# Three PSUM banks in turn for halves of the output products, maximum and bias in one VectorE operation, and another order of elements in the multiplication by the softmax reciprocals

## The chip, the core and the metric

The kernel runs on one core of one Trainium2 chip. A core has TensorE for matrix products (its results go to PSUM, 8 banks of 512 float32 per partition), VectorE, ScalarE and GpSimd for elementwise work, and SyncE, which here only issues transfers. The time is the device time of the core in microseconds; a profiled execution also gives its span, from the first to the last instruction.

## What is computed

One transformer block on 2048 rows of 576 numbers, with modulation by a conditioning vector:

```python
mod = (silu(c) @ w_mod).reshape(1, 6, 1, 576)
sa, ca, ga, sb, cb, gb = mod[:, 0], mod[:, 1], ...
h = layernorm(x) * (1 + ca) + sa
x = x + ga * attention(h)      # 32 query heads on 16 cached key/value heads, the last 512 positions
h = layernorm(x) * (1 + cb) + sb
x = x + gb * ((silu(h @ w1) * (h @ w3)) @ w2)   # 4608 hidden columns
```
In attention each query head's scores (2048 x 512) go through a softmax, are multiplied by the values, and the heads' outputs are multiplied by `wo` (4096 x 576) and summed.

## The kernel before

Everything is computed in pairs of float16 numbers, a high half and the rest: each matrix product is three products (high by high, high by low, low by high). The 2048 rows are four blocks of 512. Attention is a list of 128 slots `i`, each one query head on one block; a slot has four steps `t`, one for each tile of 128 rows. The main loop (from L1599) writes down the instructions of all engines step by step, each engine works its list in order, and the framework adds the waits between engines. In a step of slot `i` TensorE's list has:

- the scores of tile `t` (`scores`, three products of 512 columns, L508), in one of two banks tagged `S`;
- a third of the next slot's query projection (`query`, L435 and L439), in one of two banks tagged `A`;
- a part of the output products of two heads that were finished earlier (`attend_out`, `back`, L458);
- at times four transposes of normalized rows (`turn_rows`, L257) or small products of one column.

At the end of the slot come the twelve products of the probabilities of slot `i - 1` with the values (`values`, L587).

**Softmax.** VectorE takes the negated maximum of the scores (L512) and turns it into the bias of the exponential (L513), ScalarE computes the exponential from PSUM with this bias (`weights`, L525). The probabilities are split into halves by ScalarE (L557) and GpSimd (L562) and turned by a transposing transfer; the fourth tile is turned by TensorE (`turn`, L548) into a bank tagged `T`, and VectorE makes its low half (`turn_low`, L577). The reciprocals of the row sums go to memory and come back spread over the partitions as `r`, with the four tiles of a row next to each other. `normalize` (L596) multiplies the head's output `po` by them on VectorE, two slots later, at step 1; at step 3 ScalarE and GpSimd split the result (`split_on`, L606 and L607).

**Output products.** The two query heads of a key head make a pair. Its four tiles take eight steps: one for the first head (six products, both halves of the 576 columns, L458), one for the second, which adds to it. Then VectorE multiplies by a factor and adds the tile to the accumulated rows `acc` (L617). PSUM has two banks `E` for this, one for each half of the columns, so that the first product of a tile waits for the accumulate of the tile before. Small sums of peaks use free columns of the second bank (`sum_peaks`, `in_total`, `out_total`), and VectorE copies them out (L336, L1170, L1199). After the last slot `E` and a second pair of banks, in the place of `T`, take turns.

**Other uses of T.** Two banks `T` in turn serve the fourth tile and the transposes of normalized rows: for the first block before the loop (with banks `A` and `S`), for the second in the first steps (`make_h` with `early`), for the third and fourth within slots 8 to 12 and, for the second layer norm of the first two blocks, in slots 112 to 116 (`store_h`). ScalarE or VectorE reads each of them with gain and shift (L266, L268, L270, L272, L284, L286, L656). The very first query product, of slot 0, uses the first bank of `E` (`project_first`, L445 to L451).

The attention slots end at about 1590 us; then the feed-forward part runs (L874, L959). Its code stays as it is, apart from the bank and columns of the small sums.

Of the kernel before, what the change touches and what calls it, by code (L numbers as in the profile page):

```python
# [48 lines left out]
def tile_block(  # L49
# [47 lines left out]
    sc = const.tile([P, DC + 4], F32, name="sc")  # L97
    low_rows = sc[:, DC + 3 :]
# [41 lines left out]
    ones = const.tile([P, P], F32, name="ones")  # L140
    nc.gpsimd.memset(ones, 1.0)
    peak_cols = const.tile([P, 12], BF16, name="peak_cols")
# [17 lines left out]
    def mod_cols(wm, name, one, tag):  # L160

        ps = t_bank() if tag == "T" else bank(tag, f"ps_{name}")
# [12 lines left out]
    def mod_rows(wm, kind):  # L175

        vec = gate_rows[kind]
        wm = wm[0]
        for h in range(2):
            for d in (0, 3):  # L180
                nc.tensor.matmul(
                    E[:, h, :HALF], ones, wm[:, d, h * HALF : (h + 1) * HALF], start=d == 0, stop=d == 3
                )
        nc.vector.tensor_copy(half_split(vec), E[:, :, :HALF])
        return vec
# [67 lines left out]
    def turn_rows(b, m, tag):  # L253

        ps = t_bank() if tag == "T" else bank(tag, "ps_n")
        for t in range(ST):
            nc.tensor.transpose(ps[:, t * P : (t + 1) * P], norms[b][1][t][:, m * P : (m + 1) * P], ident)  # L257
        return ps
# [51 lines left out]
    factors = const.tile([P, HKV, 3], F32, name="factors")  # L310
# [17 lines left out]
    def sum_peaks(g, lo, hi, ps=None):  # L328

        ps = E[:, 1, 400:416] if ps is None else ps  # L330
        nc.tensor.matmul(ps[:, lo:hi], peak_ones, tops[g][:, lo:hi], start=True, stop=True)

    def take_sums(g, lo, hi, ps=None):

        ps = E[:, 1, 400:416] if ps is None else ps
        nc.vector.tensor_copy(peaks[g][:, 5 + lo : 5 + hi], ps[:, lo:hi])  # L336

    def score_factors(g):
        down = peaks[g][:, 5:10]
        nc.vector.tensor_scalar(  # L340
            factors[:, g, 0:2], down[:, 0:2], down[:, 2:3], score_down, op0=ALU.mult, op1=ALU.mult
        )
# [110 lines left out]
    def back(ps, o, w, t, first, last):  # L453

        rows = slice(t * P, (t + 1) * P)
        for n, (x, y) in enumerate(((0, 0), (0, 1), (1, 0))):
            for h in range(2):
                nc.tensor.matmul(  # L458
                    ps[:, h, :HALF],
                    o[:, x, rows],  # L460
                    w[:, y, h * HALF : (h + 1) * HALF],
                    start=first and n == 0,
                    stop=last and n == 2,
                )
# [35 lines left out]
    def scores(i, t):  # L500
        u, j, b = slots[i]
        g = uses[u][0]
        st = state[i]
        k, q = keys[u], st["qT"]
        rows = slice(t * P, (t + 1) * P)
        pss = bank("S", "pss")
        for n, (x, y) in enumerate(((0, 0), (0, 1), (1, 0))):
            nc.tensor.matmul(pss, q[:, x, rows], k[:, y, :], start=n == 0, stop=n == 2)  # L508
        m = (i * ST + t) % 3
        nm = nms[:, 2 * m : 2 * m + 2]  # L510
        factor = factors[:, g, j : j + 1]
        nc.vector.tensor_reduce(nm[:, 0:1], pss, axis=AX.X, op=ALU.max, negate=True)  # L512
        nc.vector.tensor_scalar(nm[:, 1:2], nm[:, 0:1], factor, P_LOG, op0=ALU.mult, op1=ALU.add)  # L513
        st["max", t] = pss, nm

    def weights(i, t):

        u, j, b = slots[i]
        factor = factors[:, uses[u][0], j : j + 1]
        st = state[i]  # L520
        pss, nm = st.pop(("max", t))
        if t == 0:
            st["l"] = odd.tile([P, 2 * ST], F32, tag="l", name="l", bufs=3)
        p = pool.tile([P, SB], F32, tag="p", name="p", bufs=PB)
        nc.scalar.activation(p, pss, AF.Exp, bias=nm[:, 1:2], scale=factor, accum_out=st["l"][:, t : t + 1])  # L525
        st["p", t] = p
# [15 lines left out]
    def turn(i, t):  # L542
# [3 lines left out]
        ps = st["t"] = t_bank().rearrange("p (j n) -> p j n", j=KC)  # L546
# [45 lines left out]
    def normalize(i):  # L592
# [16 lines left out]
    def attend_out(pair, t, j, total):  # L609
        u, _, b = slots[2 * pair]  # L610
        lane[0] += j == 0
        ps = spare()
        back(ps, state[2 * pair + j]["o"], wos[u][:, j], t, j == 0, j == 1)
        if j == 1:
# [3 lines left out]
                a, ps[:, :, :HALF], factors[:, uses[u][0], 2:3], a, op0=ALU.mult, op1=ALU.add  # L618
# [4 lines left out]
    for pair in range(n // 2):  # L623
        for k in range(2 * ST):
# [6 lines left out]
            outs.setdefault(when, []).append((pair, *divmod(k, 2)))  # L631
# [17 lines left out]
    def store_h(b, m, tag, tag_out):  # L649
# [9 lines left out]
        store_later(hd[b][m * P : m * P + n, :], hf[:n], ("s", b, m) if tag == "T" else None)  # L659
# [448 lines left out]
    def scale_first(ps):  # L1108
# [15 lines left out]
        nc.gpsimd.tensor_scalar(score_down, small[:, 5:6], SCALE / Q_DOWN, None, op0=ALU.mult)  # L1124
# [20 lines left out]
    lane = [0, ()]  # L1145

# [12 lines left out]
    def in_total(f):  # L1159

        m = peak_cols[:, 4 * (f % 2) :][:, :4]
        for part in range(2):
            peak = m[:, 2 * part + 1 : 2 * part + 2]
            nc.tensor.matmul(
                spare()[:, 1, 408:410], peak.to_broadcast([P, P]), m[:, 2 * part : 2 * part + 2],
# [3 lines left out]
    def in_taken(f):  # L1169
        nc.vector.tensor_copy(stats[:, f, :], spare()[:, 1, 408:410])  # L1170
# [24 lines left out]
    def out_total(p):  # L1195
        nc.tensor.matmul(spare()[:, 1, 410:411], peak_ones, peak_cols[:, 8 + p % 2 : 9 + p % 2], start=True, stop=True)

    def out_taken(p):
        nc.vector.tensor_copy(out_down[:, p : p + 1], spare()[:, 1, 410:411])  # L1199
# [236 lines left out]
    def make_h(b, m, early=False):  # L1436
        modulate(hT[b], m, turn_rows(b, m, "T"), vecs["shift", "a"], vecs["gain", "a"], early)
# [88 lines left out]
    at(106, 2, make_cols, "shift", "b", 3, 0.0, "T")  # L1526
    at(109, 2, make_cols, "gain", "b", 4, 1.0, "T")
    at(109, 3, lambda: spread_peaks("b", mlp_small))
    at(110, 1, lambda: scale_cols("b", t_bank(), mlp_small, 2.0**-8))
# [24 lines left out]
    turned = [turn_rows(0, m, "TTAAS"[m]) for m in range(DC + 1)]  # L1554
# [44 lines left out]
    for i in range(n + 2):  # L1599
        run(i, -1)  # L1600
        for t in range(ST):
# [121 lines left out]
```

## Time and profile before

| what | us |
|---|---|
| three runs of the kernel before: median (lowest to highest) | 2752.52 (2752.24 to 2756.41) |
| the profiled execution | 2752.42 |
| its span | 2750.3 |

In the profile's lines PE is TensorE, PEld its weight loads, DVE VectorE, ACT ScalarE, POOL GpSimd. A group's line has the source line, the engine, the operation, what it writes and reads by the program's names, the shapes and the count, then the busy time, the mean of one in ns, and the idle time of the engine just before with what ended it. A line of the list of waits has the waiting engine, tile and line, what it waited for, the total in us, how often, and the longest. A timeline line has its start, its length, and in brackets the wait before it. Products are pipelined: the end of one is modelled and lies behind the start of the next. In the table by stretches of time each line has its bounds, its length, and then the busy time of TensorE, its weight loads, VectorE, ScalarE and GpSimd.

### The profile page before, as it was taken

How to read it: one execution, taken by the hardware profiler on the slowest of the kernel's cores; microseconds unless marked ns; L12 is line 12 of the kernel's file. 1: busy time of each engine (PE TensorE's matmuls, PEld its weight loads, DVE VectorE, ACT ScalarE, POOL GpSimd, SP SyncE). 2: the span in 40 equal slices, each digit the busy share in tenths (PEclk: the TensorE clock that was granted, in tenths of full speed). 3: DMA queues.
4: the chain of work that ended last, by engine and by line, in shares of the span. 5: the costliest groups of instructions: out<-in, count | busy, mean ns of one | idle time of the engine just before them, and what ended most of it. 6: DMA issues, size and time to landing. Idle time of an engine off the chain costs nothing.

```text
span 2750.3 us, 44762 instructions
## 1 busy us (share of the span) xinstructions
PE 2682.3 (98%) x15406; PEld 1511.8 (55%) x15406; DVE 1995.2 (73%) x3550; ACT 1622.9 (59%) x3026; POOL 1873.1 (68%) x1745
## 2 busy tenths in 40 slices
PE   6899999999999999999999999999999999999998
PEld 3455555555555555555555555555555555555555
DVE  7877787878787787887876667777776666566566
ACT  6776778777777778777677635544443323333332
POOL 4677888888888877777669637688774465334435
PEclk9999999999999999999999999999999999999999
DMA  6778888778787888978879945656643434333332
GB/s 196 174 171 198 195 180 192 168 182 188 171 187 165 190 193 193 214 178 208 194 182 219 241 134 171 200 165 201 208 160 107 157 122 129 102 103 111 105 109 85
DMA packets 593460, 463.84 MB, mean 169 GB/s; under 512 B 442704, under 2 KB 472528, under 8 KB 592208
## 3 DMA queue, kind: packets, MB, share of 16 engines
q1 hardware_dynamic: 592944, 460.69, 65.4%
q8 instruction: 121, 1.98, 0.3%
q14 instruction: 107, 0.88, 0.1%
q10 hardware_dynamic: 288, 0.30, 0.0%
HBM read 264.19 MB, written 95.99 MB: 131 GB/s over the span
## 4 chain that ended last, share of the span: by engine, by line
PE 50%; DVE 2%; POOL 2%; issue 1%; DMA 1%; ACT 1%; SPq 0%; POOLq 0%; DVEq 0%; ACTq 0%
PE py L874 15%; PE px L874 11%; PE pf L959 6%; PE pe L959 6%; PE pe L458 3%; PE po L587 3%; PE pss L508 2%; PE pq L435 2%; DMA r<-row 1%; PE pt L548 0%; POOL acc L913 0%; PE pq L439 0%; DMA row<-l 0%; DVE table L512 0%; POOL sums L913 0%
## 5 line engine op out<-in xcount | busy, mean ns | idle before, releaser
L562 POOL TENSOR_TENSOR hp<-p,hp 128x512 f16<-128x512 f32 x384 | 448.8, 1171 | 269.6 <-ACT hp L557 154.1
L525 ACT ACTIVATE p<-pss,table,factors 128x512 f32<-128x512 f32 x512 | 396.8, 775 | 355.1 <-DVE table L513 175.7
L874 PEld LDWEIGHTS <-wset 128*128 128x128 f16 x3528 | 344.2, 98 | 337.4 <-issue 4.0
L512 DVE TENSOR_REDUCE table<-pss 128x1 f32<-128x512 f32 x512 | 350.3, 684 | 199.4 <-PE pss L508 198.8
L874 PE MATMUL py<-hset,wset 128*128 128x512 f16 x2016 | 482.1, 379 | 0.0
L458 PE MATMUL pe<-o 128*128 128x288 f16 x3024 | 453.4, 286 | 11.6 <-DVE acc L617 10.7
L508 PE MATMUL pss<-k,qT 128*128 128x512 f16 x1536 | 418.0, 380 | 13.2 <-ACT p L525 10.6
L458 PEld LDWEIGHTS <-o 128*128 128x128 f16 x3072 | 300.8, 98 | 186.1 <-issue 17.5
L587 PE MATMUL po<-ptw,v 128*128 128x512 f16 x1536 | 358.6, 381 | 7.8 <-DVE ptw L577 2.7
L874 PE MATMUL px<-hset,wset 128*128 128x512 f16 x1512 | 361.5, 379 | 2.1 <-ACT p L525 2.1
L94 POOL TENSOR_TENSOR akv<-u,akv 128x512 f16<-128x512 f32 x141 | 164.8, 1178 | 178.4 <-ACT akv L93 170.5
L435 PE MATMUL pq<-hT,wq 128*128 128x512 f16 x1092 | 280.6, 379 | 0.0
L557 ACT CAST hp<-p 128x512 f16<-128x512 f32 x384 | 237.3, 618 | 14.1 <-DMA ptw<-hp 0.9
L587 PEld LDWEIGHTS <-v 128*128 128x128 f16 x1536 | 147.8, 98 | 175.0 <-issue 16.2
L959 PEld LDWEIGHTS <-akv 128*128 128x128 f16 x1728 | 169.1, 98 | 89.3 <-issue 0.8
L508 PEld LDWEIGHTS <-qT 128*128 128x128 f16 x1536 | 147.6, 98 | 127.2 <-issue 14.8
L617 DVE SCALAR_TENSOR_TENSOR acc<-pe,factors,acc 128x576 f32<-128x576 f32 x252 | 204.3, 811 | 4.8 <-PE pe L458 4.8
L607 POOL TENSOR_TENSOR o<-on,o 128x512 f16<-128x512 f32 x128 | 150.2, 1174 | 54.0 <-ACT o L606 52.0
L435 PEld LDWEIGHTS <-wq 128*128 128x128 f16 x1092 | 106.9, 98 | 127.4 <-issue 1.0
L953 DVE SCALAR_TENSOR_TENSOR acc<-pf,table,acc 128x576 f32<-128x576 f32 x140 | 113.5, 811 | 79.3 <-PE pf L959 79.3
L1052 ACT COPY u<-py 128x512 f32<-128x512 f32 x72 | 42.2, 586 | 201.3 <-PE py L874 199.4
L1045 ACT ACTIVATE s<-s,table 128x512 f32<-128x512 f32 x72 | 52.0, 722 | 175.1 <-DVE s L1044 175.0
(254 smaller groups left out, 4789.0 us busy)
## 6 DMA issues: line engine op xcount, KB each, us to landing
wset<-wd SPq DMA_DIRECT2D x213, 320.0 KB, 3.2
r<-row SPq DMA_DIRECT2D x128, 256.0 KB, 3.9
oset<-od SPq DMA_DIRECT2D x106, 288.0 KB, 3.2
wraw<-in_w SPq DMA_DIRECT2D x36, 768.0 KB, 5.5
wd<-wmade SPq DMA_DIRECT2D x75, 320.0 KB, 3.2
wset<-wd SPq DMA_DIRECT2D x71, 160.0 KB, 2.2
w2raw<-in_w SPq DMA_DIRECT2D x19, 576.0 KB, 5.2
wd<-ring SPq DMA_DIRECT2D x33, 320.0 KB, 2.8
```

The costliest lines, as they stand in the source:

```text
L94: eng.tensor_sub(halves[:, 1], src, halves[:, 0])
L435: nc.tensor.matmul(ps, w[:, k // 2, m, :], hT[:, DC + m if k == 1 else m, :], start=s == 0, stop=False)
L458: nc.tensor.matmul(ps[:, h, :HALF], o[:, x, rows], w[:, y, h * HALF : (h + 1) * HALF], start=first and n == 0, stop=last and n == 2,)
L508: nc.tensor.matmul(pss, q[:, x, rows], k[:, y, :], start=n == 0, stop=n == 2)
L512: nc.vector.tensor_reduce(nm[:, 0:1], pss, axis=AX.X, op=ALU.max, negate=True)
L525: nc.scalar.activation(p, pss, AF.Exp, bias=nm[:, 1:2], scale=factor, accum_out=st["l"][:, t : t + 1])
L557: nc.scalar.copy(hp[:, 0, :], state[i]["p", t])
L562: nc.gpsimd.tensor_sub(hp[:, 1, :], state[i].pop(("p", t)), hp[:, 0, :])
L587: nc.tensor.matmul(po, v[:, x, c, :], pt[:, y, c, :], start=c == 0 and n == 0, stop=c == KC - 1 and n == 2)
L617: nc.vector.scalar_tensor_tensor(a, ps[:, :, :HALF], factors[:, uses[u][0], 2:3], a, op0=ALU.mult, op1=ALU.add)
L874: nc.tensor.matmul(ps, w[:, a, :], h[:, b, :], start=start and n == 0, stop=stop and n == 6, skip_group_check=True)
L959: nc.tensor.matmul(ps[:, h, :HALF], a[:, rows], w[:, b, :], start=m == 0, stop=m == 2)
```

## The change

1. **Three banks.** `E` is now one tile of three banks. The lower half of the columns always goes to bank 0, the upper half to bank 1 and 2 in turn (`lane[0]`, flipped by each tile). The tile `T` has one buffer instead of two. What else used `T` uses a bank of `E`: banks 1 and 2 at the start, later the one that is idle at the time (`idle()`). The small sums move to free columns of bank 0. After the last slot the two pairs `pe` and `pf` are new tiles.
2. **The order of the output products.** A step does one half of the columns for both heads (six products), the upper half first, instead of both halves for one head.
3. **One operation for maximum and bias.** L512 and L513 become one VectorE operation that adds a constant to each score, multiplies by the negated factor, takes the minimum over the row as an accumulator, and also writes the products themselves as bytes to a tile that nobody reads. It needs two more factors for each head, made at the same place as the old one.
4. **The multiplication by the reciprocals** runs over the same elements in another order: the four tiles innermost, so that `r` is read in its order in memory, and `po` and `on` in steps of 128 elements.
5. The matrix of ones is one column, read as if it were 128.

```diff
-    E = psum.tile([P, 2, 512], F32, tag="E", name="pe", bufs=1)
     turning = ExitStack()
-    tpool = turning.enter_context(tc.tile_pool(name="tpool", bufs=2, space=PSUM))
-
-    def t_bank():
-        return tpool.tile([P, 512], F32, tag="T", name="pt")
+    tpool = turning.enter_context(tc.tile_pool(name="tpool", bufs=1, space=PSUM))
+    E = tpool.tile([P, 3, 512], F32, tag="E", name="pe")
+    lane = [1, ()]
+
+    def both_halves():
+        return lane[1][lane[0] % 2][:, :, :HALF] if lane[1] else E[:, 0 : lane[0] + 1 : lane[0], :HALF]
+
+    def idle():
+        return E[:, 3 - lane[0], :]
...
-        ps = t_bank() if tag == "T" else bank(tag, "ps_n")
+        ps = idle() if tag == "E" else E[:, int(tag), :] if tag in "012" else bank(tag, "ps_n")
         for t in range(ST):
...
-    def back(ps, o, w, t, first, last):
+    def back(ps, o, w, t, h, first, last):
...
         for n, (x, y) in enumerate(((0, 0), (0, 1), (1, 0))):
-            for h in range(2):
-                nc.tensor.matmul(
-                    ps[:, h, :HALF],
-                    o[:, x, rows],
-                    w[:, y, h * HALF : (h + 1) * HALF],
-                    start=first and n == 0,
-                    stop=last and n == 2,
-                )
+            nc.tensor.matmul(
+                ps,
+                o[:, x, rows],
+                w[:, y, h * HALF : (h + 1) * HALF],
+                start=first and n == 0,
+                stop=last and n == 2,
+            )
...
-        nc.vector.tensor_reduce(nm[:, 0:1], pss, axis=AX.X, op=ALU.max, negate=True)
-        nc.vector.tensor_scalar(nm[:, 1:2], nm[:, 0:1], factor, P_LOG, op0=ALU.mult, op1=ALU.add)
+        nc.vector.tensor_tensor_reduce(
+            spent, pss, to_log.to_broadcast([P, W]), turned, 3.0e38, op0=ALU.add, op1=ALU.min, accum_out=nm
+        )
...
-            on.rearrange("d (t p) -> d t p", t=ST),
-            po.rearrange("d (t p) -> d t p", t=ST),
-            st["r"].rearrange("d p t -> d t p"),
+            on.rearrange("d (t p) -> d p t", t=ST),
+            po.rearrange("d (t p) -> d p t", t=ST),
+            st["r"],
...
-    def attend_out(pair, t, j, total):
+    def attend_out(pair, t, h, total):
         u, _, b = slots[2 * pair]
-        lane[0] += j == 0
-        ps = spare()
-        back(ps, state[2 * pair + j]["o"], wos[u][:, j], t, j == 0, j == 1)
-        if j == 1:
+        if h:
+            lane[0] = 3 - lane[0]
+        for j in range(2):
+            back(both_halves()[:, h], state[2 * pair + j]["o"], wos[u][:, j], t, h, j == 0, j == 1)
+        if not h:
             run(*total)
             a = half_split(acc[b][:, t, :])
             nc.vector.scalar_tensor_tensor(
-                a, ps[:, :, :HALF], factors[:, uses[u][0], 2:3], a, op0=ALU.mult, op1=ALU.add
+                a, both_halves(), factors[:, uses[u][0], 2:3], a, op0=ALU.mult, op1=ALU.add
             )
...
-            outs.setdefault(when, []).append((pair, *divmod(k, 2)))
+            outs.setdefault(when, []).append((pair, k // 2, 1 - k % 2))
...
-        modulate(hT[b], m, turn_rows(b, m, "T"), vecs["shift", "a"], vecs["gain", "a"], early)
+        modulate(hT[b], m, turn_rows(b, m, str(1 + m % 2) if early else "E"), vecs["shift", "a"], vecs["gain", "a"], early)
...
-            at(i + 1 + m // 3, m % 3, store_h, b, m, "T", "raw")
+            at(i + 1 + m // 3, m % 3, store_h, b, m, "E", "raw")
...
-    turned = [turn_rows(0, m, "TTAAS"[m]) for m in range(DC + 1)]
+    turned = [turn_rows(0, m, "12AAS"[m]) for m in range(DC + 1)]
...
-                    lane[1] = (E, after.tile([P, 2, 512], F32, tag="T2", name="pf"))
+                    lane[1] = tuple(after.tile([P, 2, 512], F32, tag=tag, name=tag) for tag in ("pe", "pf"))
```

The instructions' order shows three places. In these rows the number with L is the source line of the kernel in question (in the changed one L467 is `back`, L445 the query, L263 the transposes, L517 the scores, L521 the fused operation, L587 the low half of the fourth tile, L507 that of the query, L628 the accumulate), and the brackets name the engine on whose work the instruction waits.

First TensorE, where a query part ends and the second tile of an output begins. Before, this is the first head's share of both halves:

```order
L435 MATMUL pq<-hT,wq 128x512
L458 LDWEIGHTS o
L458 MATMUL pe<-o 128x288 [waits DVE_49]
L458 LDWEIGHTS o
L458 MATMUL pe<-o 128x288
```
Now it is the upper half for both heads, in a bank other than that of the first tile:

```order
L445 MATMUL pq<-hT,wq 128x512
L467 LDWEIGHTS o
L467 MATMUL pe<-o 128x288 [waits DVE_49]
L467 LDWEIGHTS o
L467 MATMUL pe<-o 128x288
```
The first product still has a wait for VectorE. Counted along VectorE's list by the values of the waits, it is in both kernels for the accumulate of the tile before, or for a small copy behind that. The first product of the lower half, a step later, has no wait of its own in either.

Second TensorE in slot 8, step 1, where a tile of the output ends and a block of normalized rows is turned. Before:

```order
L458 LDWEIGHTS o
L458 MATMUL pe<-o 128x288
L257 MATMUL pt<-ident,xn 128x128 [waits Activation_49]
L257 MATMUL pt<-ident,xn 128x128 x3
L508 LDWEIGHTS qT
```
Now:

```order
L467 LDWEIGHTS o
L467 MATMUL pe<-o 128x288
L263 MATMUL pe<-ident,xn 128x128 [waits DVE_49]
L263 MATMUL pe<-ident,xn 128x128 x3
L517 LDWEIGHTS qT
```
The transposes waited for ScalarE's reading of an earlier block in the same buffer; now they write to `pe` and wait for VectorE's accumulate of the tile whose last product stands just before them. The next output product, a step later, now waits for ScalarE's reading of these transposes.

Third VectorE in slot 7, two scores. Before:

```order
L512 TENSOR_REDUCE table<-pss 128x1 [waits PE_49]
L513 TENSOR_SCALAR table<-table,factors 128x1 [waits DVE_49]
L577 TENSOR_TENSOR ptw<-pt,ptw 128x4x128 [waits DMAHW6_49,Activation_49]
L512 TENSOR_REDUCE table<-pss 128x1 [waits PE_49]
L513 TENSOR_SCALAR table<-table,factors 128x1 [waits DVE_49]
```
Now:

```order
L521 ISA spent,table<-pss,factors 128x512 [waits PE_49]
L521 ISA table 128x1
L587 TENSOR_TENSOR ptw<-pt,ptw 128x4x128 [waits DMAHW6_49,Activation_49]
L521 ISA spent,table<-pss,factors 128x512 [waits DVE_49,PE_49]
L521 ISA table 128x1
```
The maximum and the bias are two instructions as before, the second now the read of the accumulator, which waits for nothing; the fused operation waits in some places for the one before, since all write the same tile of bytes.

More of the change, by code (lines that the diff above doesn't have):

```diff
@@ L94, in split @@
         eng.tensor_sub(halves[:, 1], src, halves[:, 0])
-    sc = const.tile([P, DC + 4], F32, name="sc")
-    low_rows = sc[:, DC + 3 :]
+    sc = const.tile([P, DC + 6], F32, name="sc")
+    low_rows, turned_down, log_up = (sc[:, DC + k : DC + k + 1] for k in (3, 4, 5))
     for r in range(0, P, 32):
@@ L139, in tile_block @@
     nc.scalar.activation(c_row, c_row, AF.Silu)
-    ones = const.tile([P, P], F32, name="ones")
+    ones = const.tile([P, 1], F32, name="ones")
     nc.gpsimd.memset(ones, 1.0)
+    ones = ones.to_broadcast([P, P])
     peak_cols = const.tile([P, 12], BF16, name="peak_cols")
@@ L160, in mod_cols @@
     def mod_cols(wm, name, one, tag):
-        ps = t_bank() if tag == "T" else bank(tag, f"ps_{name}")
+        ps = idle() if tag == "E" else bank(tag, f"ps_{name}")
         wm = wm[0]
@@ L178, in mod_rows @@
         wm = wm[0]
+        ps = both_halves()
         for h in range(2):
@@ L181, in mod_rows @@
                 nc.tensor.matmul(
-                    E[:, h, :HALF], ones, wm[:, d, h * HALF : (h + 1) * HALF], start=d == 0, stop=d == 3
+                    ps[:, h], ones, wm[:, d, h * HALF : (h + 1) * HALF], start=d == 0, stop=d == 3
                 )
-        nc.vector.tensor_copy(half_split(vec), E[:, :, :HALF])
+        nc.vector.tensor_copy(half_split(vec), ps)
         return vec
@@ L308, in load_in @@
         return raw
-    factors = const.tile([P, HKV, 3], F32, name="factors")
+    factors = const.tile([P, HKV, 7], F32, name="factors")
+    spent = const.tile([P, W], mybir.dt.uint8, name="spent")
     peaks, tops = {}, {}
@@ L509, in scores @@
         m = (i * ST + t) % 3
[L510 to L513, printed above, removed]
+        nm = nms[:, m : m + 1]
+        turned, to_log = (factors[:, g, k + j : k + j + 1] for k in (3, 5))
+        nc.vector.tensor_tensor_reduce(
+            spent, pss, to_log.to_broadcast([P, W]), turned, 3.0e38, op0=ALU.add, op1=ALU.min, accum_out=nm
+        )
         st["max", t] = pss, nm
@@ L524, in weights @@
         p = pool.tile([P, SB], F32, tag="p", name="p", bufs=PB)
-        nc.scalar.activation(p, pss, AF.Exp, bias=nm[:, 1:2], scale=factor, accum_out=st["l"][:, t : t + 1])
+        nc.scalar.activation(p, pss, AF.Exp, bias=nm, scale=factor, accum_out=st["l"][:, t : t + 1])
         st["p", t] = p
@@ L545, in turn @@
         p = st.pop(("p", t))
-        ps = st["t"] = t_bank().rearrange("p (j n) -> p j n", j=KC)
+        ps = st["t"] = tpool.tile([P, KC, P], F32, tag="T", name="pt")
         for j in range(KC):
@@ L1123, in scale_first @@
         vecs["shift", "a"], vecs["gain", "a"] = mod_a[:, 0], mod_a[:, 1]
-        nc.gpsimd.tensor_scalar(score_down, small[:, 5:6], SCALE / Q_DOWN, None, op0=ALU.mult)
+        for to, src, by in (
+            (score_down, small[:, 5:6], SCALE / Q_DOWN), (turned_down, small[:, 5:6], -SCALE / Q_DOWN),
+            (log_up, small[:, 10:11], -P_LOG * Q_DOWN / SCALE),
+        ):
+            nc.gpsimd.tensor_scalar(to, src, by, None, op0=ALU.mult)
     def scale_gate(kind, small, to):
@@ L1195, in out_total @@
     def out_total(p):
-        nc.tensor.matmul(spare()[:, 1, 410:411], peak_ones, peak_cols[:, 8 + p % 2 : 9 + p % 2], start=True, stop=True)
+        nc.tensor.matmul(spare()[:, 0, 410:411], peak_ones, peak_cols[:, 8 + p % 2 : 9 + p % 2], start=True, stop=True)
     def out_taken(p):
-        nc.vector.tensor_copy(out_down[:, p : p + 1], spare()[:, 1, 410:411])
+        nc.vector.tensor_copy(out_down[:, p : p + 1], spare()[:, 0, 410:411])
     def out_scale(p):
@@ L1525, in tile_block @@
     at(14, 2, lambda: scale_gate("b", mlp_small, mlp_gate_down))
-    at(106, 2, make_cols, "shift", "b", 3, 0.0, "T")
-    at(109, 2, make_cols, "gain", "b", 4, 1.0, "T")
+    at(106, 2, make_cols, "shift", "b", 3, 0.0, "E")
+    at(109, 2, make_cols, "gain", "b", 4, 1.0, "E")
     at(109, 3, lambda: spread_peaks("b", mlp_small))
-    at(110, 1, lambda: scale_cols("b", t_bank(), mlp_small, 2.0**-8))
+    at(110, 1, lambda: scale_cols("b", idle(), mlp_small, 2.0**-8))
     for piece in range(6):
```

21 lines of the change are left out of this document (11 added, 10 removed).

## The prediction

> **What bounds the kernel now.** I read the page's busy line first, then TensorE's rows of the timeline in the middle of attention, then the list of waits for TensorE, and last the timeline around single waits.
>
> ```profile
> span 2750.3 us, 44762 instructions
> PE 2682.3 (98%) x15406; PEld 1511.8 (55%) x15406; DVE 1995.2 (73%) x3550; ACT 1622.9 (59%) x3026; POOL 1873.1 (68%) x1745
> ```
> ```profile
> 1001.99 0.81 PE L508 MATMUL pss<-k,qT 128*128 128x512 f16 x3
> 1002.64 1.24 PE L435 MATMUL pq<-hT,wq 128*128 128x512 f16 x5
> 1003.72 0.90 PE L458 MATMUL pe<-o 128*128 128x288 f16 x6
> 1004.45 0.60 PE L548 MATMUL pt<-ident,p 128*128 128x128 f32 x4
> ```
> TensorE's starts follow each other without a hole: 0.65 us for three products of 512 columns, 0.73 us for six of 288 (0.122 us each). The change issues the same number of products in the same shapes, so only TensorE's waits can move. They are few:
>
> ```profile
> PE pe L458 <- DVE acc L617: 10.7, 11, 2.0
> PE pss L508 <- ACT p L525: 10.6, 14, 2.6
> PE po L587 <- DVE ptw L577: 2.7, 7, 0.8
> PE pe L331 <- DVE top L326: 2.6, 2, 2.1
> PE pss L508 <- ACT qT L492: 1.1, 3, 0.7
> PE pss L508 <- DVE qT L498: 0.7, 2, 0.3
> ```
> The first row is the wait at which the banks aim: output products wait until VectorE has added the tile before. The others are fed by VectorE, directly or through the exponential. Together they are 28.4 us, about 1% of the time. Each wait is somewhat longer than its row, since a product's modelled end lies behind the next one's possible start.
>
> **The banks.** By its words the change should take away the first row. The list of TensorE's instructions, shown with the change, says otherwise: the first product of a tile still waits for VectorE. Counted along VectorE's list, the value it waits for is the accumulate of the tile just before, although that one reads other columns. The three banks are one tile, and the framework keeps order by tile. So this wait stays where it was. Most of its 10.7 us also doesn't come from VectorE's own work:
>
> ```profile
> 576.76 1.06 DVE L596 TENSOR_TENSOR on<-po,r 128x512 f32<-128x512 f32 x1 [2.49 <-POOL o L607]
> 577.73 0.81 DVE L617 SCALAR_TENSOR_TENSOR acc<-pe,factors,acc 128x576 f32<-128x576 f32 x1
> ```
> ```profile
> 1501.87 1.08 DVE L596 TENSOR_TENSOR on<-po,r 128x512 f32<-128x512 f32 x1 [2.07 <-DMA r<-row]
> ```
> The accumulate stands in VectorE's queue behind the multiplication by the reciprocals (L596), which waits for GpSimd or a transfer. Of the 10.7 us I take 2 as gone.
>
> One tile also makes new waits. The transposes of the normalized rows used to go to a pool of two banks; now they go to the idle bank of the same tile.
>
> ```profile
> 142.49 0.60 PE L257 MATMUL pt<-ident,xn 128*128 128x128 f32 x4
> 144.44 0.90 PE L458 MATMUL pe<-o 128*128 128x288 f16 x6
> 145.18 0.60 PE L257 MATMUL pt<-ident,xn 128*128 128x128 f32 x4
> 146.26 0.90 PE L458 MATMUL pe<-o 128*128 128x288 f16 x6
> ```
> ```profile
> 142.74 0.82 DVE L617 SCALAR_TENSOR_TENSOR acc<-pe,factors,acc 128x576 f32<-128x576 f32 x1
> ```
> ```profile
> 144.02 0.78 ACT L272 ACTIVATE hf<-pt,mod_a 128x512 f32<-128x512 f32 x1
> 147.28 0.77 ACT L272 ACTIVATE hf<-pt,mod_a 128x512 f32<-128x512 f32 x1
> ```
> - At 142.49 the transposes followed the output products at once. Now they wait for the accumulate just issued, which ends at 143.56: 1.07 us. The two odd ones of five per block, in four blocks: 8 x 1.07 = 8.6 us.
> - The next output product, in whichever bank, waits until ScalarE has read the transposes. For the second of these groups that is 148.05 against 146.26, 1.79 us, of which the 1.07 us just lost are already given: 0.7 us. Four such places, and some tenths at the other sixteen: 4 us (0 to 9).
> - Three products for the second layer norm move into the idle bank the same way: by the same price 2 us.
>
> **Order of the products.** A step now does one half of the columns for both heads, so the second head's output is needed one step earlier.
>
> ```profile
> 339.66 0.90 PE L458 MATMUL pe<-o 128*128 128x288 f16 x6
> ```
> ```profile
> 339.88 1.15 POOL L607 TENSOR_TENSOR o<-on,o 128x512 f16<-128x512 f32 x1
> ```
> Here GpSimd's low half is ready at 341.03; the sixth product would start at 339.66 + 5 x 0.122 = 340.27, so it waits 0.8 us. I found two more such places, in the same phase of later heads (721 and 1490 us): 2 us. Elsewhere the margin holds.
>
> **The start.** The first query product goes to the same tile as two of the turned blocks, so it waits for their last reader.
>
> ```profile
> 24.90 3.57 PE L445 MATMUL pe<-hT,wq 128*128 128x512 f16 x8 [1.45 <-ACT hT L286]
> 38.20 0.60 PE L257 MATMUL pt<-ident,xn 128*128 128x128 f32 x4
> ```
> ```profile
> 26.74 0.79 ACT L286 ACTIVATE hf<-pt,mod_a 128x512 f32<-128x512 f32 x1
> ```
> ```profile
> 38.81 0.80 DVE L268 TENSOR_SCALAR hT<-pt,mod_a 128x512 f16<-128x512 f32 x1
> ```
> It starts at 27.53 instead of 24.90, 2.6 us later. These eight products took 0.42 us each (3.57 us to the last one's modelled end), twice the later pace, and I expect that again, while the operands of the last products, late before, are then ready: 2 us remain. The early transposes alternate banks, but now each waits for the readers of the one before: at 38.20 until 39.61, 1.4 us. VectorE's own backlog behind it hides about 1 us of both. I take 2.5 us (0 to 4).
>
> **The fused maximum.** A reduction and a small operation become one operation with an accumulator, whose read is a second instruction.
>
> ```profile
> 1003.37 0.68 DVE L512 TENSOR_REDUCE table<-pss 128x1 f32<-128x512 f32 x1
> 1004.09 0.21 DVE L513 TENSOR_SCALAR table<-table,factors 128x1 f32<-128x1 f32 x1
> 1004.22 0.17 DVE L532 RECIPROCAL l<-l 128x4 f32<-128x4 f32 x1
> ```
> ```profile
> 18.54 0.76 DVE L128 SCALAR_TENSOR_TENSOR wc<-wc,gate_b 128x576 f32<-128x576 f32 x1
> 19.22 0.08 DVE L128 DVE_READ_ACCUMULATOR wc<-wc,gate_b 128x1 f32 x1
> 19.22 0.76 DVE L128 SCALAR_TENSOR_TENSOR wmr<-wmr,gate_b 128x576 f32<-128x576 f32 x1
> ```
> ```profile
> L498 DVE SCALAR_TENSOR_TENSOR qT<-pq,qT 128x512 f16<-128x512 f32 x127 | 87.6, 690 | 64.1 <-ACT qT L492 63.7
> L596 DVE TENSOR_TENSOR on<-po,r 128x512 f32<-128x512 f32 x128 | 138.9, 1085 | 18.6 <-POOL o L607 10.1 <-DMA r<-row 6.6 <-PE po L587 1.8
> L1053 DVE TENSOR_TENSOR u<-px,u 128x512 f32<-128x512 f32 x72 | 49.8, 691 | 100.7 <-ACT u L1052 90.3 <-DMA wset<-wd 4.5 <-POOL ring L797 2.8
> L340 DVE TENSOR_SCALAR factors<-us,sc 128x2 f32<-128x2 f32 x16 | 9.0, 562 | 0.0
> ```
> The pair holds VectorE 0.85 us (1003.37 to 1004.22). The trace shows no such fused operation. The nearest rows are two-input operations on 512 columns from PSUM (690 ns), and one with an accumulator, whose read costs the queue nothing (both rows at 19.22) and whose overlap saves 0.08. So 0.61 us: 0.24 x 512 = 123 us less on VectorE, less 2 x 16 x 0.56 = 18 us for the two new factors. Bounds: 0.61 and 0.85, and more if the operation takes several cycles per element (a rival). ScalarE gets its bias 0.24 us earlier. VectorE's load in attention:
>
> ```profile
> 100.00:850.00 750.00, 736.71 (x4217) 412.64 (x4216) 594.49 (x1199) 576.68 (x1112) 614.67 (x595) 1.00 0.80 180
> 850.00:1600.00 750.00, 734.21 (x4238) 413.95 (x4236) 564.23 (x1136) 551.78 (x1075) 562.67 (x523) 1.00 0.85 199
> ```
> The fifth number is VectorE's busy time: 1158.7 of 1500 us, 77%; 105 us less over about 1580 makes it 70%. What it gives TensorE: of the 17.7 us of waits below the first row I take 14 as gone with the hidden part, as most are well under 1 us and stand behind two to four such pairs in VectorE's queue; with the 2 us above, 16 us (0 to 25).
>
> **The multiplication by the reciprocals.** L596 takes 1085 ns, L1053 with the same sizes and memories 691; what differs is that L596 reads r at every fourth element. The new form reads r in order, and reads PSUM and writes SBUF in steps of 128 elements instead. No row has that. Bounds 691 and 1085 + 394 = 1479; I take 1085, as the stride is only moved. 128 x 0.39 = 50 us of VectorE either way, perhaps 4 us of TensorE's waits. [...]
>
> **Sum.** +8.6 + 4 + 2 (idle bank) + 2 (second head) + 2.5 (start) + 1 (the factors, where VectorE is late) - 16 = +4; less 1 us for waits of transposes on their own pool that go: +3. The profiled execution took 2752.4 us (2750.3 span), the median is 2752.5: 2755. A measurement of this kernel can tell about 0.2% from no change, 5.5 us; this is within.
>
> **Rivals.**
> - *VectorE's relief carries further* (25%). At 70% of attention every lag behind it shrinks, L596 comes to 691, and ScalarE's faster start lets GpSimd clear its backlog. For it: 16 of 28 us is all I gave. Against: long waits hang on GpSimd. All 28 us gone, and the costs, with only the 8.6 fixed and the rest at two thirds, at 16: 2740.
> - *The fused operation is no shorter than the pair* (27%), the slower side. It isn't in the trace; at 0.85 us its gain is nil and the costs of 20 us stand alone: 2772. That is the point from which the kernel is slower; below 0.75 us it is level. [...] At twice the time, 1.22 us, VectorE would have 0.37 x 512 = 189 us more to do, near 90% of attention, and the score waits would grow as well: 2800 or more (5 of the 27). [...]
> - *The banks do come apart* (6%): the accumulate is always long done where the wait stands, and the products never stop for it. -10.7 and the 16, and the costs halved to 10, since the transposes then go freely too: 2736. [...] Against: the wait in the list.
>
> **How the numbers follow.** Forecast 42%, rivals 25, 27 and 6. The forecast's own range is 2746 to 2764, wide enough to reach past both bounds. Faster: rivals one and three and a little less for their tails, 0.29; slower: rival two and the forecast's upper tail, 0.33; same 0.38. The range 2736 to 2778 leaves out the deep ends of each rival.
>
> **What would show it.** Right: the row of output products on the accumulate keeps 8 us or more; a new row of transposes on the accumulate with 6 to 8 waits of about 1 us; the first query product near 27.5 us; fused operation plus read at about 0.61 us from start to start; fewer and shorter score waits. Wrong: the output products without waits on VectorE, a fused operation above 0.75 us, L596's successor far from 1085 ns, or new waits on ScalarE or GpSimd above 10 us.

## The result and the profile after

The changed kernel takes 2769.03 us (median of 5 runs, 2768.74 to 2770.19), beside 2754.33 us for the kernel before on the same chip: ratio 1.0051, 95% interval 1.0040 to 1.0062. It is slower by about 15 us. The profiled execution took 2769.09 us, its span is 2767.2 us, 16.9 more than before.

The page's busy line of the changed kernel:

```profile
span 2767.2 us, 45342 instructions
...
PE 2683.5 (97%) x15406; PEld 1511.3 (55%) x15406; DVE 1941.1 (70%) x3582; ACT 1623.2 (59%) x3026; POOL 1873.2 (68%) x1747
```
TensorE does the same work, VectorE 54 us less (1995.2 to 1941.1), and the kernel is still slower. So TensorE waits longer. To see how much, I took the time from the start of each product to the start of the next, less its pace (0.216 us for 512 columns, 0.1225 for 288, 0.109 for a transpose, about 0.03 for the few narrow ones). That excess is 88.6 us before and 105.4 after, and the 16.8 between them is the difference of the spans. It lies at the start (first 100 us: 33.0 to 36.3) and in attention (100 to 1600 us: 45.3 to 57.8); the rest is nearly level (10.3 to 11.2).

The list of waits for TensorE in the changed kernel (total in us, times, longest):

```profile
PE pss L517 <- ACT p L535: 13.2, 17, 2.4
...
PE pe L467 <- DVE acc L628: 8.5, 12, 2.2
PE pe L263 <- DVE acc L628: 6.0, 6, 1.1
...
PE pe L455 <- ACT hf L292: 3.8, 1, 3.8
...
PE pe L467 <- POOL o L617: 2.6, 3, 1.1
PE pe L467 <- ACT hf L667: 2.6, 2, 1.7
...
PE pe L467 <- ACT hf L278: 1.6, 2, 0.9
...
PE pe L263 <- DVE table L1183: 1.1, 1, 1.1
...
PE pe L263 <- DVE us L343: 1.1, 1, 1.1
```
The output products still wait for the accumulate (8.5 us, 10.7 before). New are the transposes L263 that wait for VectorE, eight of them in the three rows with L628, L1183 and L343, and the products that wait for ScalarE's reading of the transposes (L667, L278) and for GpSimd (L617). The score wait on the exponential has not shrunk but grown, from 10.6 to 13.2.

TensorE, VectorE and ScalarE at the place that the prediction showed at 142 us:

```profile
146.26 0.66 PE L263 MATMUL pe<-ident,xn 128*128 128x128 f32 x4 [0.98 <-DVE acc L628]
...
148.26 0.90 PE L467 MATMUL pe<-o 128*128 128x288 f16 x6
149.00 0.60 PE L263 MATMUL pe<-ident,xn 128*128 128x128 f32 x4
...
151.13 0.90 PE L467 MATMUL pe<-o 128*128 128x288 f16 x6 [0.89 <-ACT hf L278]
```
```profile
145.39 0.82 DVE L628 SCALAR_TENSOR_TENSOR acc<-pe,factors,acc 128x576 f32<-128x576 f32 x1
```
```profile
150.31 0.77 ACT L278 ACTIVATE hf<-pe,mod_a 128x512 f32<-128x512 f32 x1
```
The transposes start when the accumulate of another bank ends (145.39 + 0.82 = 146.21), and the output product at 151.13 starts when ScalarE has read the transposes in a bank that the product doesn't write (151.08).

The second head's output comes late by the new order of the products, here for the sixth of six:

```profile
349.13 0.78 PE L467 MATMUL pe<-o 128*128 128x288 f16 x5
351.01 0.30 PE L467 MATMUL pe<-o 128*128 128x288 f16 x1 [1.10 <-POOL o L617]
```
```profile
349.80 1.15 POOL L617 TENSOR_TENSOR o<-on,o 128x512 f16<-128x512 f32 x1
```
The first query product starts at 26.62 instead of 24.90:

```profile
26.62 3.57 PE L455 MATMUL pe<-hT,wq 128*128 128x512 f16 x8 [3.83 <-ACT hf L292]
```
The fused operation on VectorE, and its groups (busy us, mean ns of one, idle before):

```profile
1012.49 0.74 DVE L521 CUSTOM_DVE_ANT_0 spent<-pss,factors 128x512 uint8<-128x512 f32 x1
1013.15 0.08 DVE L521 DVE_READ_ACCUMULATOR2_ANT table<- 128x1 f32 x1
1013.15 0.17 DVE L542 RECIPROCAL l<-l 128x4 f32<-128x4 f32 x1
```
```profile
L521 DVE CUSTOM_DVE_ANT_0 spent<-pss,factors 128x512 uint8<-128x512 f32 x512 | 381.4, 745 | 252.1 <-PE pss L517 250.4
...
L606 DVE TENSOR_TENSOR on<-po,r 128x512 f32<-128x512 f32 x128 | 136.0, 1063 | 19.5 <-POOL o L617 12.4 <-DMA r<-row 5.2 <-PE po L597 1.8
...
L350 DVE TENSOR_SCALAR factors<-us,sc 128x2 f32<-128x2 f32 x48 | 23.4, 546 | 0.0
```
It holds VectorE 0.66 us (1012.49 to 1013.15), where the pair held it 0.85. The read of the accumulator costs the queue nothing: the next operation starts with it, at 1013.15. The multiplication by the reciprocals is level (1063 ns, 1085 before). The factor operations take 23.4 us in all instead of 9.0.

### The profile page after: what moved, and what is told of

The parts are those of the page before. It is cut to its first block, busy times and chain, and to the rows that moved or that the text cites. A ratio compares the mean times of both kernels' runs of the same rounds, so it can differ in the third digit from the quotient of the medians.

```text
span 2767.2 us, 45342 instructions
## 1 busy us (share of the span) xinstructions
PE 2683.5 (97%) x15406; PEld 1511.3 (55%) x15406; DVE 1941.1 (70%) x3582; ACT 1623.2 (59%) x3026; POOL 1873.2 (68%) x1747
## 5 line engine op out<-in xcount | busy, mean ns | idle before, releaser
L521 DVE CUSTOM_DVE_ANT_0 spent<-pss,factors 128x512 uint8<-128x512 f32 x512 | 381.4, 745 | 252.1 <-PE pss L517 250.4
L467 PE MATMUL pe<-o 128*128 128x288 f16 x3024 | 453.7, 286 | 17.1 <-DVE acc L628 8.5
L517 PE MATMUL pss<-k,qT 128*128 128x512 f16 x1536 | 418.6, 380 | 15.2 <-ACT p L535 13.2
L467 PEld LDWEIGHTS <-o 128*128 128x128 f16 x3072 | 300.7, 98 | 191.6 <-issue 22.0
L445 PE MATMUL pq<-hT,wq 128*128 128x512 f16 x1092 | 281.3, 380 | 0.0
L517 PEld LDWEIGHTS <-qT 128*128 128x128 f16 x1536 | 147.7, 98 | 129.5 <-issue 18.7
L628 DVE SCALAR_TENSOR_TENSOR acc<-pe,factors,acc 128x576 f32<-128x576 f32 x252 | 204.2, 810 | 17.6 <-PE pe L467 9.0
L617 POOL TENSOR_TENSOR o<-on,o 128x512 f16<-128x512 f32 x128 | 149.7, 1169 | 56.1 <-ACT o L616 54.2
L445 PEld LDWEIGHTS <-wq 128*128 128x128 f16 x1092 | 107.1, 98 | 127.5 <-issue 1.4
L964 DVE SCALAR_TENSOR_TENSOR acc<-pe,table,acc 128x576 f32<-128x576 f32 x140 | 113.5, 811 | 79.2 <-PE pe L970 79.2
```

The source lines that it names most:

```text
L445: nc.tensor.matmul(ps, w[:, k // 2, m, :], hT[:, DC + m if k == 1 else m, :], start=s == 0, stop=False)
L467: nc.tensor.matmul(ps, o[:, x, rows], w[:, y, h * HALF : (h + 1) * HALF], start=first and n == 0, stop=last and n == 2,)
L521: nc.vector.tensor_tensor_reduce(spent, pss, to_log.to_broadcast([P, W]), turned, 3.0e38, op0=ALU.add, op1=ALU.min, accum_out=nm)
L628: nc.vector.scalar_tensor_tensor(a, both_halves(), factors[:, uses[u][0], 2:3], a, op0=ALU.mult, op1=ALU.add)
```

## The experiments

All times are medians, beside the kernel before run on the same chip (2754.73, 2755.25 and 2754.21 us in the three groups). Single executions spread more: in the first group those of the kernel before lie between 2750.3 and 2758.4 us. Two questions were open. Where did the relief of VectorE go? And do the banks cost what they cost because they are one tile?

**The parts alone.** *The fused operation*, put into the kernel before: items 3 and 5 of the change only.

```diff
...
-        nc.vector.tensor_reduce(nm[:, 0:1], pss, axis=AX.X, op=ALU.max, negate=True)
-        nc.vector.tensor_scalar(nm[:, 1:2], nm[:, 0:1], factor, P_LOG, op0=ALU.mult, op1=ALU.add)
+        nc.vector.tensor_tensor_reduce(
+            spent, pss, to_log.to_broadcast([P, W]), turned, 3.0e38, op0=ALU.add, op1=ALU.min, accum_out=nm
+        )
...
```


> The kernel before with the fused maximum and bias alone (and its two further factors); the banks and the order of the products stay. Theory A (a shorter VectorE step gives TensorE little, since the long score waits end with ScalarE's list and the further factors stand ahead of maxima): 0 to 4 us faster, output products waiting on the accumulate still 8 us or more. Theory B (the relief of the prediction is real and the banks ate it): 12 to 16 us faster. Theory C (the fused operation itself is the harm): 3 us slower or more.

2751.86 us, ratio 0.9989 (0.9978 to 0.9999): 3 us faster. B and C fall.

*The banks and the order of the products*: the changed kernel without its items 3 and 4.

> The changed kernel with the old pair of maximum and bias and the old order in the multiplication by the reciprocals, so that only the banks and the order of the products differ from the kernel before. Theory A: 17 to 23 us slower than before, with eight waits of about 1.1 us of transposes on VectorE. Theory B: 28 to 33 us slower, since the whole would then be this less 16. Theory C: 10 us slower or less.

2772.79 us, ratio 1.0067 (1.0055 to 1.0080): 18 us slower, as A says. Its list of waits has the rows of the banks:

```profile
PE pss L514 <- ACT p L531: 10.5, 15, 2.6
...
PE pe L464 <- DVE acc L624: 9.0, 8, 2.3
PE pe L263 <- DVE acc L624: 6.0, 6, 1.1
```
*The order of the multiplication*, alone in the kernel before:

```diff
...
-            st["r"].rearrange("d p t -> d t p"),
...
+            st["r"],
```
(and `on` and `po` as `d p t`).

> The kernel before with only the new order of elements in the multiplication by the reciprocals. Its duration was 1085 ns and was 1063 in the changed kernel, so theories A, B and C all say the same: 0 to 1 us faster, not distinguishable from no change; anything beyond 3 us would be a term that all of them miss.

2751.40 us, ratio 0.9989 (0.9981 to 0.9998). That is 3 us, a little more than expected; in its profile the operation takes 1060 ns, 25 ns less, and TensorE's excess is only 1.1 us less than before. The rest of the 3 us lies in what it is compared with: the profiled execution of the kernel before took 2752.42 us, 2.3 less than the median of this group. So the traces show a gain of about 1 us; the interval leaves up to 5 open.

**The further factors.** In the changed kernel the two further factor operations of a head went to GpSimd:

```diff
-            nc.vector.tensor_scalar(
+            (nc.gpsimd if at_ else nc.vector).tensor_scalar(
                 factors[:, g, at_ : at_ + 2], small[:, 0:2], small[:, 2:3], by, op0=ALU.mult, op1=ALU.mult
             )
```


> The changed kernel with the two further factors of each head made by GpSimd instead of VectorE. Theory A: the two score waits of 1.20 us at 420 and 802 us fall back to about 0.3, the whole 2 to 4 us faster than the changed kernel, 2765 to 2767. Theories B and C: no difference, 2768 to 2770, since the factors are seldom in the way.

2759.73 us, ratio to the kernel before 1.0019 (1.0010 to 1.0028), so 9.3 us faster than the changed kernel: more than twice what A expected. The place at 415 us shows why. VectorE, GpSimd and TensorE in the changed kernel:

```profile
415.39 3.46 DVE L350 TENSOR_SCALAR factors<-us,sc 128x2 f32<-128x2 f32 x3
418.76 0.74 DVE L521 CUSTOM_DVE_ANT_0 spent<-pss,factors 128x512 uint8<-128x512 f32 x1
```
```profile
415.19 1.16 POOL L572 TENSOR_TENSOR hp<-p,hp 128x512 f16<-128x512 f32 x1
416.31 1.40 POOL L851 TENSOR_TENSOR w2raw<-w2raw,gate_b 128x576 f32<-128x576 f32 x1
417.67 1.16 POOL L617 TENSOR_TENSOR o<-on,o 128x512 f16<-128x512 f32 x1
```
```profile
420.51 0.81 PE L517 MATMUL pss<-k,qT 128*128 128x512 f16 x3 [1.04 <-ACT p L535]
```
Three operations on two elements take 3.46 us. Each ends just when a GpSimd operation ends: at 416.3, 417.7 and 418.8. The maximum of the scores stands behind them in VectorE's queue, the exponential behind the maximum, and TensorE waits for the bank. The same place with the two operations on GpSimd:

```profile
414.98 0.98 DVE L350 TENSOR_SCALAR factors<-us,sc 128x2 f32<-128x2 f32 x1
415.87 0.74 DVE L521 CUSTOM_DVE_ANT_0 spent<-pss,factors 128x512 uint8<-128x512 f32 x1
```
```profile
418.90 0.81 PE L517 MATMUL pss<-k,qT 128*128 128x512 f16 x3
```
The wait is gone. In the thirteen groups of factors that lie after 300 us, VectorE spends 21.4 us in the changed kernel and 6.2 us here. TensorE's excess in the 10 us from the start of each of them falls from 13.1 to 3.8 us. These 9.3 us account for the difference (9.3 by the medians, 8.2 between the two profiled spans). 6.2 of them lie at the six places where GpSimd held up two or all three operations, 3.1 at the seven others.

*The same in the kernel before*, with the fused operation:

> The kernel before with the fused maximum and bias, the two further factors made by GpSimd. Theory D (the shorter VectorE step is worth some 10 us by itself, and three factor operations in a row on VectorE give most of it back): 7 to 11 us faster than before, score waits on the exponential about 5 us instead of 11. Theory A (the relief is little in any case): 1 to 5 us faster, no more than the fused operation with its factors on VectorE.

2741.39 us, ratio 0.9952 (0.9938 to 0.9965): 14 us faster than before. That is more than D's 7 to 11, and the score waits fall to 7.6 us, not to 5. So D holds in its direction and was too low in its number, and A's reason (that the relief is little in any case) falls. The list of waits:

```profile
PE pe L463 <- DVE acc L623: 9.1, 10, 2.3
PE pss L513 <- ACT p L531: 7.6, 8, 2.4
```
*One element instead of two.* This asks whether the price comes from GpSimd or from the number of operations. The edit is shown against the kernel with the fused operation alone:

```diff
-            nc.vector.tensor_scalar(
-                factors[:, g, at_ : at_ + 2], small[:, 0:2], small[:, 2:3], by, op0=ALU.mult, op1=ALU.mult
-            )
+            for k in range(2):
+                nc.vector.tensor_scalar(
+                    factors[:, g, at_ + k : at_ + k + 1], small[:, k : k + 1], small[:, 2:3], by,
+                    op0=ALU.mult, op1=ALU.mult,
+                )
```


> The kernel before with the fused maximum and bias, and with each head's three factor operations on two elements written as six operations on one element, all on VectorE. Theory G (an operation of VectorE on two elements waits for the end of the GpSimd operation that is running, one on one element doesn't): each takes 0.15 to 0.25 us wherever GpSimd is, and the whole comes near the kernel with these factors on GpSimd, 2740 to 2746, 9 us or more faster than before. Theory H (it is the number of VectorE's operations ahead of a maximum): twice as many, so no faster than with two elements, 2751 or more.

2749.52 us, ratio 0.9983 (0.9974 to 0.9991). VectorE and GpSimd at the same place, and the group of all 96:

```profile
403.35 1.16 DVE L346 TENSOR_SCALAR factors<-us,sc 128x1 f32<-128x1 f32 x6
404.42 0.74 DVE L519 CUSTOM_DVE_ANT_0 spent<-pss,factors 128x512 uint8<-128x512 f32 x1
```
```profile
403.15 1.16 POOL L570 TENSOR_TENSOR hp<-p,hp 128x512 f16<-128x512 f32 x1
404.27 1.41 POOL L848 TENSOR_TENSOR w2raw<-w2raw,gate_b 128x576 f32<-128x576 f32 x1
```
```profile
L346 DVE TENSOR_SCALAR factors<-us,sc 128x1 f32<-128x1 f32 x96 | 18.5, 261 | 0.0
```
The hardware part of G holds: six operations on one element pass in 1.07 us (403.35 to 404.42) while GpSimd's operations run. Its forecast of the time doesn't, and H's bound isn't reached either. At the six places where GpSimd was in the way, TensorE's excess falls from 6.1 us to nothing; at the seven others, where six operations (1.07 us) hold VectorE longer than the three did (0.55 to 0.85), it rises from 6.7 to 9.0. With the operations on GpSimd it is 0 and 3.8. So what counts is VectorE's time right ahead of a maximum, and how much of it the place can hide: the same 1.07 us costs nothing at the six places.

**The banks as tiles.** Three tiles of one bank each in the changed kernel; VectorE's accumulate becomes two:

```diff
-    E = tpool.tile([P, 3, 512], F32, tag="E", name="pe")
+    Es = [tpool.tile([P, 512], F32, tag=f"E{k}", name=f"pe{k}") for k in range(3)]
...
-            nc.vector.scalar_tensor_tensor(
-                a, both_halves(), factors[:, uses[u][0], 2:3], a, op0=ALU.mult, op1=ALU.add
-            )
+            for k in range(2):
+                nc.vector.scalar_tensor_tensor(
+                    a[:, k], both_halves()[k], factors[:, uses[u][0], 2:3], a[:, k], op0=ALU.mult, op1=ALU.add
+                )
```


> The changed kernel with three tiles of one bank each in the place of one tile of three banks; the accumulate becomes two operations of 288 columns, one after the other, since an operation cannot cross tiles. Theory E (order is kept by tile, and that is what makes the banks' part slow): the eight waits of transposes on the accumulate, the waits of products on ScalarE's reading and most of the products' waits on the accumulate go, 15 to 22 us faster than the changed kernel, 2747 to 2754, less up to 4 us for VectorE, whose accumulates take about 0.2 us more each. Theory F (these waits come from a VectorE and a ScalarE that are late, whatever the tiles): 2766 to 2772.

2759.28 us, ratio to before 1.0015 (1.0007 to 1.0024): 9.8 us faster than the changed kernel. Its transposes follow the output products at once again, at the place that showed the wait at 146.26:

```profile
148.11 0.90 PE L470 MATMUL pe<-o 128*128 128x288 f16 x6
148.84 0.60 PE L266 MATMUL pe<-ident,xn 128*128 128x128 f32 x4
```
Its list of waits has no row of transposes on the accumulate, one single wait of an output product on it, and longer ones that hang on VectorE:

```profile
PE pss L520 <- ACT p L538: 19.1, 23, 2.4
...
PE po L600 <- DVE ptw L590: 5.0, 10, 0.6
...
PE pe L470 <- DVE acc L632: 1.1, 1, 1.1
```
```profile
L632 DVE SCALAR_TENSOR_TENSOR acc<-pe,factors,acc 128x288 f32<-128x288 f32 x504 | 235.5, 509 | 16.0 <-PE pe L470 8.5
```
So E holds for the accumulate: order is kept by tile, and that made these waits. Products still wait 2.7 us for ScalarE's reading (1.4 and 1.3 us in the list, 4.2 in the changed kernel): after a turned block its bank is the next tile's, whatever the tiles. The gain is smaller than E's 15 us. Two accumulates of 288 columns take 2 x 0.51 us instead of 0.81, VectorE's work rises by 36 us, and the waits that hang on VectorE rise (13.2 to 19.1, 1.6 to 5.0).

Where the gain lies is another thing than E expected. TensorE's excess falls by 6.5 us in the first 100 us (36.3 to 29.8) and by only 3.3 in attention (57.8 to 54.5). The first query product no longer shares a tile with the turned blocks. The other traces agree on the start: in the first 100 us the excess is 29.3 to 34.5 us in the eight kernels whose turned blocks have banks of their own, 35.6 to 39.2 in the three with one tile of three banks, and 29.8 and 30.2 in the two with three tiles. So the start with one tile is about 5 us longer. The clock granted in these 100 us differs as well (0.88 in the changed kernel, 0.91 in the kernel before; 0.86 to 0.88 in those three, 0.88 to 0.97 in the ten others), and no run separates the two. In attention the longer waits behind VectorE take back most of what the tiles give.

*With the factors on GpSimd as well*:

> The changed kernel with three tiles of one bank, two accumulates of 288 columns, and the further factors by GpSimd. From the parts (10 us from the tiles and 9 from the factors, against the changed kernel): 2748 to 2752. If the two gains are the same waits: 2756 to 2759.

2747.41 us, ratio 0.9975 (0.9965 to 0.9986), just below the 2748 to 2752 of the parts: the two gains add.

*Two tiles, half accumulates*: banks and turned blocks as before, half of the columns in a step, and each half accumulated in its own step, once alone and once with the rest (the fused operation, the further factors on GpSimd, the new order of the multiplication). The accumulate, shown against the changed kernel:

```diff
-        if not h:
-            nc.vector.scalar_tensor_tensor(
-                a, both_halves(), factors[:, uses[u][0], 2:3], a, op0=ALU.mult, op1=ALU.add
-            )
+        a = half_split(acc[b][:, t, :])[:, h]
+        nc.vector.scalar_tensor_tensor(
+            a, both_halves()[h], factors[:, uses[u][0], 2:3], a, op0=ALU.mult, op1=ALU.add
+        )
```


> As the kernel with two tiles and half accumulates, but with the old maximum and bias and the old multiplication, so that only the output products differ from the kernel before. Theory E: 5 to 11 us faster than before, 2744 to 2750. Theory F, or VectorE's 50 us more in the way of the scores: within 3 us of before or slower.

> The fused operation with factors by GpSimd and the new order of the multiplication, but with two tiles of one bank each for the output products, half a tile's columns a step, and each half accumulated right after its six products; the turned blocks keep their two banks. Theories D and E together: the accumulate of a half is a whole step old when its bank is written again, so the waits on it (10 to 13 us) go nearly all, and no new ones come at the turned blocks: 15 to 22 us faster than before, 2732 to 2740. Theory F, or VectorE's additional 50 us for the half accumulates in the way: 2742 to 2750.

Alone 2759.94 us (1.0016, 1.0007 to 1.0025), with the rest 2745.59 us (0.9964, 0.9952 to 0.9977). Both miss what E forecast and come where VectorE's additional work was said to put them. The list of waits of the first:

```profile
PE pss L517 <- ACT p L534: 9.2, 12, 1.8
PE po L596 <- DVE ptw L586: 9.1, 13, 1.6
PE pss L517 <- DVE qT L507: 5.4, 8, 1.3
PE pe L467 <- DVE acc L627: 4.7, 6, 1.2
...
PE pf L467 <- DVE acc L627: 2.7, 3, 1.4
```
The wait for the accumulate nearly goes where E said it would: in the slots 1.2 us of 10.7 are left. The other 3.5 of the 4.7, and the 2.7 on `pf`, come after the last slot (from 1595 us on), where the two halves are again one tile; the kernel before has no such wait there. VectorE's 46 us more (1995.2 to 2041.2) come back in two rows that were small before: ptw 2.7 to 9.1, qT 0.7 to 5.4. TensorE's excess says how much each part counts: it is 2.5 us more than before in attention and 4.9 more after 1600 us. So most of what this version loses lies at its end, and its time came where F had put it partly for another reason.

**A version that beats both**: the kernel before, with the fused operation, all factors on GpSimd, and the new order of the multiplication.

> A version put together: the kernel before with the fused maximum and bias, all three factor operations of a head on GpSimd, and the new order of the multiplication; banks and order of products as before. From the single parts: 14 us for the fused operation with factors by GpSimd, up to 3 for the order, 1 to 2 for the third factor operation: 16 to 19 us faster than before, 2736 to 2739. If the parts don't add (the waits that are left hang on GpSimd and transfers): 2740 to 2743.

2740.91 us, ratio 0.9949 (0.9937 to 0.9961), 13 us faster than before and 28 faster than the changed kernel. That is in the 2740 to 2743 expected if the parts don't add. It is not distinguishable from the fused operation with two factors on GpSimd (2741.39); the order and the third factor add nothing that shows.

## Why the prediction was right in part and wrong in part

The measured 2769.0 lies in the range (2736 to 2778) and on the side that had 0.33. The likeliest time, 2755, was 14 us too low, and its case, no change, did not come. That the range holds the time is in part luck: its upper part was there for a fused operation no shorter than the pair, and that did not come either.

| step of the sum | predicted | measured | from |
|---|---|---|---|
| transposes wait for the accumulate | +8.6 | +8.2 | rows L263 on L628, L1183, L343: 6.0 + 1.1 + 1.1 |
| next output product waits for ScalarE | +4 | +4.2 | rows L667 and L278 |
| products for the second layer norm | +2 | +0.9 | one new wait on L628 |
| second head's output | +2 | +2.6 | row L617, three places, as forecast |
| start | +2.5 | +3.3 | excess of the first 100 us in the two profiled executions; about 5 over all traces |
| transposes' waits on their own pool go | -1 | -0.2 | row L257 on ptw L577 of the kernel before |
| shorter VectorE step (with the multiplication) | -16 | -13 | banks alone, 2772.8, to factors on GpSimd, 2759.7 |
| the two further factors | +1 | +9.3 | factors on GpSimd, 2759.7, to the changed kernel |

**The banks** were forecast right, place by place; only the start was taken too low. The first query product began at 26.62 us, between its old 24.90 and the 27.53 forecast, and the rest of the start lost more than the term allowed. That the wait on the accumulate stays, since the three banks are one tile, was argued from the waits in the list; the three tiles have now shown it. With a tile for each bank they came free one by one: of the 8.5 us of output products and the 6.0 us of transposes that waited on the accumulate, a single wait of 1.1 us is left. The parts 8.6 + 4 + 2 + 2 + 2.5 are 19, the banks alone cost 18. The measured column adds up to 15.3, and 14.7 was measured; its rows come from single profiled executions and from medians, so a closer match would be chance.

**The fused operation** is shorter than the pair, by 0.19 us instead of 0.24. Its rival (no shorter, 2772) comes near the measured time, but by the wrong mechanism: at 0.66 us it is below the 0.75 at which that rival called the kernel level. No run shows twice the time, 1.22 us, from which that rival's 2800 was worked out; 0.66 was measured. The relief of 16 us is 13, so its size was nearly right.

**The step that failed** is "+ 1 (the factors, where VectorE is late)". The prediction had their cost on VectorE nearly right (18 us forecast; 23.4 - 9.0 = 14.4 measured), from the row of L340 with its mean of 562 ns. It then treated this as load, to be set against the 123 us that the fused operation saves, and added 1 us; 9.3 were measured. But a saved microsecond of VectorE isn't worth the same everywhere. From the banks alone to the factors on GpSimd, VectorE's busy time falls by 69 us (1995.4 to 1926.1) for 13 us of the kernel: 0.2 for each. The factors stand right ahead of a maximum, where the score bank is waited for: 15.2 us there cost 9.3, 0.6 for each. The mean of 562 ns was a warning as well: in the kernel before, six of the sixteen took 258 to 277 ns, with no GpSimd operation beside them, and each of the ten longer ones (370 to 1233 ns) ended within 0.03 us of the end of one.

The changed kernel has 48 of these operations: 28 took 258 to 286 ns, where GpSimd rested or was about to end an operation, and 20 took 371 to 1446 ns, each ending within 0.03 us of the end of a GpSimd operation. So three in a row can each meet another operation of GpSimd. At four places all three did and at two more two of them, and there they held VectorE for 1.6 to 3.4 us. That the ends coincide is measured; what couples the two engines is not shown. The prediction didn't weigh it.

**The multiplication** stays as forecast, at 1063 ns (1085 before). What its reads in order and its accesses in steps of 128 elements each cost, no run separates.

## What to carry to other kernels

Price a small operation by where it stands: here one in front of the work that the busiest engine waits for cost 0.6 of its length, while time saved elsewhere on the same engine returned a fifth. Before adding small VectorE operations, compare the shortest and the longest of the same kind in the trace; a spread as here, from 0.26 to 1.2 us, is a reason to see whether the long ones end with a GpSimd operation. One-element operations (six in 1.07 us), or GpSimd itself, avoided it here. Banks that shall come free one by one have to be tiles of their own in this framework, and then count what it costs the reader that can no longer take them in one operation (here 2 x 0.51 us instead of 0.81).

## What the runs showed of the hardware

- Of the 48 VectorE operations on two elements (L350) in the changed kernel, 28 took 258 to 286 ns, with GpSimd at rest or just ending an operation; the 20 that took longer, up to 1446 ns, each ended within 0.03 us of the end of a GpSimd operation. On one element (L346 in the kernel with six single operations) the mean of 96 was 261 ns, and six passed in 1.07 us while GpSimd worked.
- The fused add, multiply and minimum over 512 columns of PSUM held the queue 0.66 us in the changed kernel, and the read of its accumulator (82 ns) hid entirely: the operation behind it started with it.
- An accumulate of 288 columns took 509 ns (the kernel with three tiles), one of 576 columns 810 (the changed kernel): halving the columns saved 0.30 us of 0.81.
